# Query projections of batches 2 and 3 as three float32r products, and a newly searched issue order

## The chip, the cores and the metric

The kernel runs on one core of one Trainium2 chip. The metric is device microseconds of one execution; three executions of the kernel before took 582.05, 582.50 and 582.72 us (median 582.5).

## The reference, cut to what matters

Three layers follow one another, on 4 batches of 576 positions (2304 tokens of 512 numbers), all in float32.

1. Performer attention, 8 heads of 64, taken in 4 pairs of heads per batch. With `proj = x @ omega.T` (128 features) each of q and k becomes `exp(proj - max)`. For k the maximum is taken per position over the features and then `kv = k_p.T @ v`; for q too, and the output is `q_p @ kv` over its normalizer.
2. A dense layer: `h = x @ w_in`, `g = h * clip(h + 3, 0, 6) / 6`, `x = g @ w_out` (512 to 2048 to 512).
3. A mixture of 8 experts (512 to 1024 to 512, one expert per token, many tokens skipped): `x + gate * relu(x @ w1[e]) @ w2[e]`.

The change touches the product `proj` of q in batches 2 and 3, the second product of the expert with few rows left ("small expert"), and the order of everything.

## The kernel before, in words

The attention works on pairs (b, p): batch b, heads 2p and 2p+1. A [128 x 576] tile holds the 64 numbers of the two heads on partitions 0 to 63 and 64 to 127, so each product with `wb` (omega, scaled) uses one half of the rows of TensorE's array. For one pair: `load_k`, `load_q`, `load_v` fetch it (L417 to L430); `phi_mm` (L452) projects k; `phi_max`, `phi_exp` make its features; `k_kvs` (L489) sums them with v; `q_proj` (L511 to L531) projects q, in two calls of 288 positions, each one product per head into a PSUM bank of its own; `q_copy` (L547, ACT) moves the result to SBUF; `q_max` (L555, POOL) takes the maximum over partitions, `q_sub` (L560, DVE) and `q_exp` (L564, ACT) finish the features; `x_nums` (L574), `x_div`, `x_turn` (L596) give the attention's output, and `x_hi`, `x_lo` split it into two float32r parts `xh`, `xl`.

Tiles with tag `raw` hold k and q of a pair. There are three such buffers, and in the kernel before a pair uses two.

The dense layer runs over five chunks of tokens (512, 512, 256, 512, 512) and 16 blocks f of the hidden width. `mm1(c, f)` (L716) makes 12 float32r products (xh·wh, xl·wh, xh·wl, over four slices of 128), DVE and ACT make g and split it into `gh` and `gl`, `mm2(c, f, t)` (L747) adds three products of 512 columns to an accumulator. While chunk 0 runs, `w_in` and `w_out` are converted and split by ACT and DVE (`cv_*`, L643 to L695). Batches 0 and 1 of the attention precede and accompany chunk 0; batches 2 and 3 accompany chunks 1 and 2. The expert layer stands at the end: one expert with up to 576 rows (`ga_*`, L1038 and L1070), and up to 32 rows of another, the small expert (`s_*`): `s_up` (L1173), `s_turn_r` (L1184), `s_down` (L1191 to L1197, 8 steps of 4 products, each on 32 columns of the array).

Nothing is scheduled on the chip: the program adds some 2,090 pieces of work with an engine, dependences and tiles to a planner, and a stored list of numbers, ORDER, gives the order in which they are issued; each engine takes its own pieces in that order. The planner's costs and due times only served the search for that list, and the number of idle products that keep TensorE busy in batch 0 (`fill`, L295) comes from its gaps. The lines around the change:

```python
for r in range(2):
    T.matmul(ps[r][:, 0:n], wb[half(r), :], qr[half(r), c], start=True, stop=True)
```

TensorE works in three shapes here: the full array (the dense layer, the experts, transposes), the array cut into two halves of rows (`phi_mm`, `q_proj`), and cut into strips of columns (`k_kvs`, `x_nums`, `s_up`, `s_down`). A step from one shape to another is called a turn below. The planner gives a turn 0.2 us.

Of the kernel before, what the change touches and what calls it, by code (L numbers as in the profile page):

```python
# [9 lines left out]
F32 = mybir.dt.float32  # L10
# [37 lines left out]
QPE = ()  # L48
# [3 lines left out]
MERGE = 2  # L52
VX = 2
# [200 lines left out]
def performer_moe_kernel(  # L254
# [59 lines left out]
    ones = const.tile([128, 128], BF16, name="ones")  # L314
    V.memset(ones, 1.0)

    first = const.tile([128, 1], F32, name="first")
    G.partition_all_reduce(first, idle[:, 0:1], channels=128, reduce_op=bass_isa.ReduceOp.max)
    half_t = const.tile([128, 1], F32, name="half_t")
    V.memset(half_t, 0.5)  # L320
# [1334 lines left out]
```

## Time and profile before

| | |
|---|---|
| median of three runs | 582.5 us (582.05 to 582.72) |
| the profiled execution | 580.91 us, its span 579.1 us |
| granted TensorE clock, mean | 0.997 of 2.4 GHz |
| busy: PE, DVE, ACT, POOL | 98%, 73%, 51%, 19% of the span |

The span runs from the first to the last instruction; 1.8 us of the profiled execution lie around it. PE is TensorE's stream of products, PEld its weight loads. A float32 product is issued as two instructions, a float32r product as one. The end of a product is modelled, so durations overlap; what one costs is read from the distance of starts.

### The profile page before, as it was taken

The page shows a single profiled execution, that of the slowest core. Times are in us where ns is not written, and L with a number is a line of the kernel's source. Part 1 is how long each engine was busy: PE and PEld are TensorE (multiplying, and loading weights), DVE is VectorE, ACT ScalarE, POOL GpSimd, SP SyncE. Part 2 cuts the span into 40 slices and gives each one's busy share as a digit, 9 for nine tenths or more (in the row PEclk, how much of TensorE's full clock was granted, in tenths as well). Part 3 has the DMA queues.
Part 4 walks back from the last instruction along what each step waited for, and adds up shares of the span by engine and source line. Part 5 has one row for each costly group of instructions (what it writes and reads, how often), then busy time and mean ns, then how long its engine had stood idle before and what let it go on. Part 6 is the DMA issues. An engine that isn't in the chain of part 4 may idle for free. (4 is left out here: it accounts for less than half of the span.)

```text
span 579.1 us, 11188 instructions
## 1 busy us (share of the span) xinstructions
PE 565.2 (98%) x4115; PEld 468.8 (81%) x4115; DVE 423.5 (73%) x1116; ACT 293.6 (51%) x665; POOL 109.5 (19%) x83
## 2 busy tenths in 40 slices
PE   9899999999999999999999999999999999999993
PEld 7778788888888787878988888888888888898872
DVE  5999999988652441356678886798899974599962
ACT  6999999896573533357743431321432224553310
POOL 4543023000020202023222000020020133200363
PEclk9999999999999999999999999999999999999998
DMA  8634665656465143214544243132123435264721
GB/s 329 214 112 162 206 217 184 210 187 223 163 236 153 37 136 119 60 51 124 180 140 153 74 126 100 47 92 55 37 38 105 149 93 163 85 229 133 237 65 66
DMA packets 37256, 79.52 MB, mean 137 GB/s; under 512 B 5612, under 2 KB 6252, under 8 KB 37200
## 3 DMA queue, kind: packets, MB, share of 16 engines
q1 hardware_dynamic: 35312, 74.93, 41.1%
q0 software_dynamic: 1744, 3.56, 2.0%
q8 instruction: 33, 0.54, 0.4%
q10 hardware_dynamic: 144, 0.29, 0.2%
q14 instruction: 23, 0.19, 0.1%
HBM read 63.71 MB, written 15.18 MB: 136 GB/s over the span
## 5 line engine op out<-in xcount | busy, mean ns | idle before, releaser
L747 PE MATMUL acc<-wo,gh 128*128 128x512 f32 x576 | 180.8, 395 | 0.0
L747 PEld LDWEIGHTS acc<-wo,gh 128*128 128x128 f32 x576 | 105.5, 188 | 22.1 <-issue 1.2
L767 DVE CUSTOM_DVE_ANT_0 idle<-x,wg 128x512 uint8<-128x512 f32 x162 | 112.7, 695 | 5.3 <-ACT x L753 1.5
L747 PE MATMUL acc<-wo,gl 128*128 128x512 f32 x288 | 112.3, 390 | 0.0
L555 POOL PARTITION_ALL_REDUCE mx<-pr x26 | 52.9, 2076 | 237.1 <-ACT pr L547 237.1
L731 ACT CAST gh<-g 128x512 fp32r<-128x512 f32 (+1 forms) x80 | 46.6, 584 | 97.0 <-PE acc L747 80.7
L737 DVE TENSOR_TENSOR gl<-g,gh 128x512 fp32r<-128x512 f32 (+1 forms) x80 | 51.2, 640 | 57.1 <-ACT gh L731 21.7
L722 ACT ACTIVATE g<-mm,half_t 128x512 f32<-128x512 f32 (+1 forms) x80 | 52.0, 651 | 67.7 <-DVE gl L737 36.1
L716 PE MATMUL mm<-xh,wih 128*128 128x512 f32 (+1 forms) x320 | 80.8, 374 | 0.2 <-DVE xn L587 0.2
L716 PE MATMUL mm<-xl,wih 128*128 128x512 f32 (+1 forms) x320 | 78.9, 368 | 0.0
L727 DVE SCALAR_TENSOR_TENSOR g<-g,mm 128x512 f32<-128x512 f32 (+1 forms) x80 | 49.6, 630 | 26.1 <-ACT g L722 25.8
L716 PEld LDWEIGHTS mm<-xh,wih 128*128 128x128 f32 x320 | 56.0, 188 | 11.7 <-DVE g L727 0.6
L716 PEld LDWEIGHTS mm<-xl,wih 128*128 128x128 f32 x320 | 56.9, 188 | 10.2
L747 PEld LDWEIGHTS acc<-wo,gl 128*128 128x128 f32 x288 | 54.0, 188 | 11.7
L716 PE MATMUL mm<-xh,wil 128*128 128x512 f32 (+1 forms) x256 | 61.6, 363 | 0.0
L716 PEld LDWEIGHTS mm<-xh,wil 128*128 128x128 f32 x256 | 44.9, 189 | 7.5
L845 POOL DMA_INDIRECT tab<-rec,r_sloti x18 | 19.3, 1070 | 154.5 <-DVE rec L841 150.6
L473 ACT ACTIVATE kp<-att,kmx 128x128 f32<-128x128 f32 x130 | 38.3, 390 | 7.8 <-DVE kmx L458 6.7
L458 DVE TENSOR_REDUCE kmx<-att 128x3 f32<-128x384 f32 (+1 forms) x64 | 28.8, 483 | 12.4 <-PE att L452 12.2
L560 DVE TENSOR_TENSOR pr<-pr,mx 128x576 f32<-128x576 f32 x26 | 26.1, 1005 | 1.4 <-POOL mx L555 1.3
L672 DVE CUSTOM_DVE_ANT_0 ca<-w,ca 128x1024 uint16<-128x1024 uint16 x32 | 23.6, 741 | 3.0 <-ACT w L658 2.2
L452 PEld LDWEIGHTS att<-wb,raw 64*128 64x128 f32 x260 | 19.8, 190 | 5.6 <-ACT pr L547 1.5
(222 smaller groups left out, 773.8 us busy)
## 6 DMA issues: line engine op xcount, KB each, us to landing
wil<-wils SPq DMA_DIRECT2D x64, 256.0 KB, 2.7
w<-w_in SPq DMA_DIRECT2D x16, 512.0 KB, 3.7
w<-w_out SPq DMA_DIRECT2D x16, 512.0 KB, 3.5
out<-x SPq DMA_DIRECT2D x18, 256.0 KB, 3.3
x1d<-x SPq DMA_DIRECT2D x18, 256.0 KB, 3.9
vx<-vn SPq DMA_DIRECT2D x13, 322.5 KB, 4.0
wils<-cl SPq DMA_DIRECT2D x16, 256.0 KB, 2.9
wraw<-w SPq DMA_DIRECT2D x16, 256.0 KB
```

Source lines behind the costliest of these rows:

```text
L458: V.reduce_max(out=mx[:, 0:n], in_=st[key, b, p, g, h][:, 0:n * M].rearrange("p (g m) -> p g m", m=M), axis=AX.X, negate=True)
L473: A.activation(kp[:, i], ps[:, i * M:(i + 1) * M], AF.Exp, bias=mx[:, i:i + 1], scale=1.0)
L555: G.partition_all_reduce(mx, st["e", b, p, r], channels=128, reduce_op=bass_isa.ReduceOp.max)
L560: V.tensor_sub(pr, pr, st.pop(("qm", b, p, r)))
L672: V.tensor_tensor(c, c, lo, op=ALU.add)
L716: T.matmul(po, w[:, k, :], moving(x, k, c), start=(n == 0), stop=(n == 3 * KC - 1))
L722: A.activation(t, mmp[c, f][:, 0:CHS[c]], AF.Relu, bias=half_t, scale=2.0 ** -UP / 6.0)
L727: V.scalar_tensor_tensor(out=t, in0=t, scalar=1.0, in1=mmp.pop((c, f))[:, 0:CHS[c]], op0=ALU.min, op1=ALU.mult)
L731: A.copy(gh, gt[c, f])
L737: V.tensor_sub(gl, t, gh.bitcast(F32))
L747: T.matmul(accs[c, t], g[:, ts], w[:, r, f % 2, :], start=(f == 0 and j == 0), stop=(f == FT - 1 and j == 2))
L767: V.tensor_tensor_reduce(out=idle.bitcast(mybir.dt.uint8), in0=x1[i], in1=wg[:, e, :], scale=1.0, scalar=0.0, op0=ALU.mult, op1=ALU.add, a ...
```

## The change

It does three things.

First, in batches 2 and 3 the projection of q is made of parts. `wb_hi` and `wb_lo` split `wb` once into `wbh` and `wbl`; per pair `q_hi` (ACT) rounds q to float32r and `q_lo` (DVE) takes the rest. `q_proj` then issues three float32r products per head, wbh·qh, wbl·qh and wbh·ql, instead of one float32 product, in calls of 320 and 256 positions instead of 288 and 288. `qh` and `ql` are tiles of tag `raw`, of which there are still three. So when `q_lo` runs, q, qh and ql hold all three, and `load_k` of the next pair is put behind `q_lo` (`aft`).

Second, small tiles share memory to make room for the new ones (`r_pos` with `r_d`, the list's work tiles in the buffer of `wbh`, `ea` and `ra` in one tile, and the like).

Third, ORDER is a new list. Read against the names of the pieces, the two lists differ in these points:

| | before | after |
|---|---|---|
| pieces in all; on ACT; on DVE | 2090; 557; 651 | 2108; 566; 660 |
| turns before the first `mm1` | 14 | 19 |
| turns from there to `mm1(1, 0)` | 18 | 15 |
| turns from there to the experts | 40 | 42 |
| turns in the experts' stretch | 4 | 6 |
| PE pieces ahead of the first `mm1` | 53 | 55 |
| `s_down`, 8 steps | all in a row | 3, then `ga_down(7, 2)`, then 5 |
| `wb_hi` | - | third of all pieces |
| `wb_lo` | - | at `mm1(0, 12)` |
| `table` (DVE, two memsets) | at `mm1(0, 10)` | at `mm1(1, 13)` |

Around the pairs (3, 0) and (3, 1) the new list has, on PE: `phi_mm(3,0)` first half and second half, `mm2(1,14)`, `x_nums(2,3)`, `q_proj(3,0)` twice, `route_rank`, `x_turn(2,3)`, `k_kvs(3,0)`, `phi_mm(3,1)`; on DVE, in that stretch: `q_sub(2,3)`, two `phi_max(3,0)`, `q_lo(3,0)`; on SP `load_k(3,1)` stands right behind `x_nums(2,3)`. The core of the diff, without the list:

```diff
+    wbh = sm.tile([128, M], F32R, tag="wbh", name="wbh")
+    wbl = od.tile([128, M], F32R, tag="wbl", name="wbl")
...
+        if b >= SPLIT:
+            return (slice(0, 320), slice(320, S))[i]
...
+    def wb_hi():
+        A.copy(wbh, wb)
+    def wb_lo():
+        V.tensor_sub(wbl, wb, wbh.bitcast(F32))
+    def q_hi(b, p):
+        st["qh", b, p] = at.tile([128, S], F32R, tag="raw", bufs=RAW, name="qh")
+        A.copy(st["qh", b, p], st["qr", b, p])
+    def q_lo(b, p):
+        st["ql", b, p] = at.tile([128, S], F32R, tag="raw", bufs=RAW, name="ql")
+        V.tensor_sub(st["ql", b, p], st["qr", b, p], st["qh", b, p].bitcast(F32))
...
-        if (b, p) not in QPE:
+        if b >= SPLIT:
+            qh, ql = st["qh", b, p], st["ql", b, p]
+            for j, (w, x) in enumerate(((wbh, qh), (wbl, qh), (wbh, ql))):
+                for r in range(2):
+                    T.matmul(ps[r][:, 0:n], w[half(r), :], x[half(r), c], start=(j == 0), stop=(j == 2))
+        elif (b, p) not in QPE:
...
+            add("ACT" if b + p == 0 else "SP", SPC, -9, load_k, (), seq="sraw", w=["kr"], tl=[("raw", "k")], nbytes=S * 512,
+                aft=[("ql", (b * 4 + p - 1) // 4, (p - 1) % 4)] if b * 4 + p > 4 * SPLIT else [])
...
+            fine = b >= SPLIT
+            if fine:
+                add("ACT", act(S), u, q_hi, (), r=["qr"], w=["qh"], tl=[("raw", 0), ("raw", "h")])
+                add("DVE", dve(S), u, q_lo, (), mode="x", r=["qh", "wbl"], w=["ql"], tl=[("raw", 0), ("raw", "h"), ("raw", "l")])
...
+                add("PE", 3 * (n + 32) / 2400 + 0.03 if fine else 0.62, u + i, q_proj, (i,), mode="r", r=["wb", "ql" if fine else "qr"] + ["qm", "shapes"] * mine, w=[("qps", i)],
+    sc.add("ACT", 0.22, 90.0, lambda: wb_hi(), r=["wb"], w=["wbh"])
+    sc.add("DVE", 0.2, 90.0, lambda: wb_lo(), mode="x", r=["wbh"], w=["wbl"])
```

## Rows read from the trace of the kernel before

**Rows 1.** The page's first part: busy time, share of span, instructions.

```profile
PE 565.2 (98%) x4115; PEld 468.8 (81%) x4115; DVE 423.5 (73%) x1116; ACT 293.6 (51%) x665; POOL 109.5 (19%) x83
```

**Rows 2.** Busy time by stretch: length, PE, PEld, DVE, ACT, POOL, clock, DMA share, GB/s.

```profile
0.00:20.00 20.00, 17.75 (x166) 14.54 (x168) 13.81 (x29) 14.62 (x42) 9.57 (x10) 1.00 0.86 310
20.00:40.00 20.00, 17.61 (x350) 14.60 (x348) 19.15 (x44) 18.91 (x57) 11.00 (x6) 1.00 0.48 153
40.00:60.00 20.00, 19.98 (x231) 16.64 (x227) 19.39 (x44) 19.20 (x49) 4.44 (x2) 1.00 0.50 159
...
165.00:306.00 141.00, 141.00 (x1302) 116.95 (x1300) 70.40 (x152) 71.12 (x190) 27.67 (x14) 1.00 0.39 119
...
560.00:580.00 20.00, 10.00 (x105) 8.07 (x104) 4.92 (x9) 1.48 (x4) 6.56 (x7) 0.88 0.18 65
```

**Rows 3.** Timeline of PE, first `mm1`: start us, us, engine, line, operation, tiles, count.

```profile
47.40 1.19 PE L716 MATMUL mm<-xh,wih 128*128 128x512 f32 x4
```

**Rows 4.** Timeline of PE, batch 3.

```profile
268.28 0.39 PE L747 MATMUL acc<-wo,gl 128*128 128x512 f32 x1
268.51 0.49 PE L596 MATMUL att<-ident,xn 128*128 128x128 f32 x3
268.93 1.24 PE L519 MATMUL att<-raw,wb 64*128 64x288 f32 x8
270.01 1.53 PE L452 MATMUL att<-wb,raw 64*128 64x128 f32 x20
271.47 0.28 PE L489 MATMUL att<-vx,kp 128*64 128x65 f32 x2
```

**Rows 5.** Timeline of PE around calls that stand alone, and float32 transposes on the full array.

```profile
255.04 0.62 PE L747 MATMUL acc<-wo,gh 128*128 128x512 f32 x2
255.49 0.39 PE L747 MATMUL acc<-wo,gl 128*128 128x512 f32 x1
255.81 1.24 PE L519 MATMUL att<-raw,wb 64*128 64x288 f32 x8
...
303.00 0.76 PE L519 MATMUL att<-raw,wb 64*128 64x288 f32 x4
303.69 0.74 PE L747 MATMUL acc<-wo,gh 128*128 128x512 f32 x2
...
500.04 0.99 PE L994 MATMUL att<-ident,xga 128*128 128x128 f32 x8
500.96 0.73 PE L747 MATMUL acc<-wo,gh 128*128 128x512 f32 x2
```

**Rows 6.** Timeline of PE: float32r products of 320 and of 256 columns.

```profile
540.17 0.75 PE L1038 MATMUL mm<-xl,gw 128*128 128x320 f32 x4
540.75 0.75 PE L1038 MATMUL mm<-xh,gw 128*128 128x320 f32 x4
541.34 0.62 PE L1070 MATMUL acc<-gw,grh 128*128 128x512 f32 x2
...
546.09 0.64 PE L1038 MATMUL mm<-xl,gw 128*128 128x256 f32 x4
546.57 1.12 PE L1038 MATMUL mm<-xh,gw 128*128 128x256 f32 x8
```

**Rows 7.** Instructions of L519: count, duration ns min/median/max, first and last start.

```profile
L519 PEld LDWEIGHTS att<-raw,wb x96: 182/186/188, 30.9 to 305.4; 64*128 64x128 f32 x96
```

**Rows 8.** Groups by shape, 165 to 306 us: count, busy, mean ns, idle before.

```profile
L564 ACT ACTIVATE pr<-pr 128x576 f32<-128x576 f32 x14 | 9.6, 695 | 3.8 <-DVE pr L560 3.0 <-DVE rd L585 0.7
...
L560 DVE TENSOR_TENSOR pr<-pr,mx 128x576 f32<-128x576 f32 x14 | 14.3, 1019 | 0.8 <-POOL mx L555 0.7
L737 DVE TENSOR_TENSOR gl<-g,gh 128x512 fp32r<-128x512 f32 x15 | 10.4, 691 | 24.2 <-PE acc L747 10.0 <-PE att L596 7.1 <-ACT gh L731 6.9
```

**Rows 9.** Timeline of PE, then of PEld, around the small expert's second product.

```profile
561.94 2.48 PE L1196 MATMUL acc<-ew,rT 128*32 128x128 f32 x64
564.35 0.73 PE L1070 MATMUL acc<-gw,xh 128*128 128x512 f32 x2
...
561.94 1.45 PEld L1196 LDWEIGHTS acc<-ew,rT 128*32 128x32 f32 x52
563.76 0.39 PEld L1196 LDWEIGHTS acc<-ew,rT 128*32 128x32 f32 x12 [0.37 <-issue]
```

**Rows 10.** The loads of k: time from issue to landing, and one issue on SP.

```profile
DMA to landing us min/median/max: 2.9/4.3/6.4
...
264.68 0.33 SPq L419 DMA_DIRECT2D raw<-kt  x1
```

More of the change, by code (lines that the diff above doesn't have):

```diff
@@ L52 @@
 MERGE = 2
+SPLIT = 2
 VX = 2
@@ L315, in performer_moe_kernel @@
     V.memset(ones, 1.0)
-    first = const.tile([128, 1], F32, name="first")
-    G.partition_all_reduce(first, idle[:, 0:1], channels=128, reduce_op=bass_isa.ReduceOp.max)
+    const.tile([128, 1], F32, name="even")
+    upper = const.tile([128, 1], F32, name="upper")
+    G.partition_all_reduce(upper, idle[:, 0:1], channels=128, reduce_op=bass_isa.ReduceOp.max)
     half_t = const.tile([128, 1], F32, name="half_t")
@@ L328, in performer_moe_kernel @@
     pidx = const.tile([128, 1], F32, name="pidx")
-    upper = const.tile([128, 1], F32, name="upper")
     thr = const.tile([128, NT // 128], F32, name="thr")
@@ L361, in performer_moe_kernel @@
     od = ctx.enter_context(tc.tile_pool(name="od", bufs=1))
-    od.tile([128, 56], F32, tag="pad", name="pad")
+    wbh = sm.tile([128, M], F32R, tag="wbh", name="wbh")
+    wbl = od.tile([128, M], F32R, tag="wbl", name="wbl")
+    od.tile([128, 8], F32, tag="pad", name="pad")
     at = ctx.enter_context(tc.tile_pool(name="at", bufs=1))
@@ L815, in route_copy @@
         V.tensor_copy(tot, ps[:, 64:64 + TPC[c] * NE].rearrange("p (n e) -> p n e", e=NE))
-        pos = sm.tile([128, TPC[c], NE], F32, tag="r_pos", name="r_pos")
+        pos = sm.tile([128, TPC[c], NE], F32, tag="r_d", name="r_pos")
         V.tensor_copy(pos, ps[:, 0:TPC[c] * NE].rearrange("p (n e) -> p n e", e=NE))
@@ L822, in route_slot @@
         tot, pos, oh, act = rt["tot"], rt["pos"], rt["oh"], rt["act"]
-        sm_ = sm.tile([128, TPC[c]], F32, tag="r_sm", name="r_sm")
+        sm_ = sm.tile([128, TPC[c]], F32, tag="r_mx", name="r_sm")
         V.reduce_sum(out=sm_, in_=rt["ex"], axis=AX.X)
@@ L872, in list_in @@
         j3 = bc(jdx.unsqueeze(2), LS)
-        exc = sm.tile([128, NE], F32, tag="l_exc", name="l_exc")
+        lw = lb["w"] = sm.tile([128, M], F32, tag="wbh", name="lw")
+        exc = lw[:, 3 * NL:3 * NL + NE]
         V.tensor_sub(exc, inc, nb)
@@ L883, in list_e @@
         ge, lt = lb["ge"], lb["lt"]
-        hit = sm.tile([128, NL], F32, tag="l_hit", name="l_hit")
+        lw = lb["w"]
+        hit = lw[:, 0:NL]
         V.reduce_sum(out=hit, in_=ge, axis=AX.X)
         V.tensor_mul(lt, ge, bc(eidx.unsqueeze(1), LS))
-        ei = sm.tile([128, NL], I32, tag="lb_e", name="lb_e")
-        eb = sm.tile([128, NL], F32, tag="l_eb", name="l_eb")
+        ei = lw[:, NL:2 * NL].bitcast(I32)
+        eb = lw[:, 2 * NL:3 * NL]
         V.reduce_sum(out=eb, in_=lt, axis=AX.X)
@@ L902, in list_r @@
         V.tensor_scalar(hit, hit, -float(TABN), float(TABN), op0=ALU.mult, op1=ALU.add)
-        ri = sm.tile([128, NL], I32, tag="lb_r", name="lb_r")
+        ri = lb["w"][:, 3 * NL + NE:4 * NL + NE].bitcast(I32)
         V.tensor_add(ri, eb, hit)
@@ L1207, in performer_moe_kernel @@
     ntot = sm.tile([128, 1], I32, tag="ntot", name="ntot")
-    ea = sm.tile([128, 1], I32, tag="ea", name="ea")
-    ra = sm.tile([128, 1], I32, tag="ra", name="ra")
-    es = sm.tile([128, 1], I32, tag="es", name="es")
-    rs = sm.tile([128, 1], I32, tag="rs", name="rs")
+    ear = sm.tile([128, 2], I32, tag="ea", name="ear")
+    ea, ra = ear[:, 0:1], ear[:, 1:2]
+    esr = sm.tile([128, 2], I32, tag="es", name="esr")
+    es, rs = esr[:, 0:1], esr[:, 1:2]
     lb = {}
@@ L1257, in list_b @@
         V.tensor_sub(rest, cnt, used)
-        nb = begun(rest, "b_nb")
-        lb["nb"], lb["inc"] = nb, prefix(nb, "b_inc")
+        nb = begun(rest, "a_oh")
+        lb["nb"], lb["inc"] = nb, prefix(nb, "a_t8")
     def expert_of(t):
@@ L1305, in attention, with add @@
             t = start + p * period + AT[f"o{b}{p}"]
-            def add(eng, cost, dt, f, a, r=(), w=(), tl=(), nbytes=0, seq=None, mode="f", over=()):
+            def add(eng, cost, dt, f, a, r=(), w=(), tl=(), nbytes=0, seq=None, mode="f", over=(), aft=()):
                 last = chain.get(seq)
@@ L1312, in add @@
                     chain[seq] = (seq, b, p)
-                sc.add(eng, cost, t + dt, lambda p=p: f(b, p, *a), mode=mode, o=[last] if last else [], r=[k if k in ("wb", "shapes") else (k, b, p) if isinstance(k, str) else (*k, b, p) for k in r],
+                sc.add(eng, cost, t + dt, lambda p=p: f(b, p, *a), mode=mode, o=[*([last] if last else []), *aft], r=[k if k in ("wb", "wbl", "shapes") else (k, b, p) if isinstance(k, str) else (*k, b, p) for k in r],
                        w=[(k, b, p) if isinstance(k, str) else (*k, b, p) for k in w] + list(over),
@@ L1318, in kind @@
                 return "ps"
-            add("ACT" if b + p == 0 else "SP", SPC, -9, load_k, (), seq="sraw", w=["kr"], tl=[("raw", "k")], nbytes=S * 512)
+            add("ACT" if b + p == 0 else "SP", SPC, -9, load_k, (), seq="sraw", w=["kr"], tl=[("raw", "k")], nbytes=S * 512,
+                aft=[("ql", (b * 4 + p - 1) // 4, (p - 1) % 4)] if b * 4 + p > 4 * SPLIT else [])
             add("SP", SPC, -9, load_q, (), seq="sraw", w=["qr"], tl=[("raw", 0)], nbytes=S * 512)
@@ L1356, in attention @@
                 n = c.stop - c.start
-                add("PE", 0.62, u + i, q_proj, (i,), mode="r", r=["wb", "qr"] + ["qm", "shapes"] * mine, w=[("qps", i)],
-                    tl=[("raw", 0)] + [(kind("x"), "q", r, i) for r in range(2)] + [("pr", r) for r in range(2)] +
+                add("PE", 3 * (n + 32) / 2400 + 0.03 if fine else 0.62, u + i, q_proj, (i,), mode="r", r=["wb", "ql" if fine else "qr"] + ["qm", "shapes"] * mine, w=[("qps", i)],
+                    tl=([("raw", "h"), ("raw", "l")] if fine else [("raw", 0)]) + [(kind("x"), "q", r, i) for r in range(2)] + [("pr", r) for r in range(2)] +
                     ([("qmx", g, h) for g, h in parts] if mine else []))
```

163 rows, old and new, of the table ORDER are left out of this document.

## The prediction, made before the result was known

> **What bounds the kernel.** I read the busy shares first, then the same by stretches, then TensorE's timeline where the change touches it. PE is busy for 565.2 of 579.1 us, DVE for 73% and ACT for 51% [rows 1]. By stretches there are two regimes. In the first 40 us PE sits idle for 4.6 us and spends more on idle products, while ACT and DVE are close to full from 20 us on; from 40 us to the end of the products, at about 570 us, PE hardly rests [rows 2]. The granted clock is at the upper level, 2.4 GHz, in these stretches. So from 47.4 us on, the first `mm1` [rows 3], time is what PE's stream costs: a product removed is gained, and work added to ACT or DVE costs nothing unless PE must wait for it. In batches 2 and 3 (165 to 306 us) DVE and ACT are each busy for half of the 141 us [rows 2].
>
> **1. `q_proj` in batches 2 and 3: 8 pairs, 16 calls.** Before, the eight instructions of two calls run from 268.93 to 270.01, 1.08 us [rows 4]. About 0.1 of that is the turn into half-array shape, so a call is 0.49 us and a pair 0.98. That the two heads run side by side is seen in this: twenty float32 instructions of 128 columns on half arrays (`phi_mm`) start within 1.46 us, 0.073 each with a turn in it, where eight on the full array take 0.92 us, 0.115 each [rows 4, 5].
>
> After, a call is three products on each half. The trace has no float32r product on a half array. The nearest rows are float32r products on the full array: four of 320 columns in 0.58 us, so 0.146 each, four of 256 in 0.48 us, 0.12 each [rows 6]. If the halves run side by side as they do in float32, a pair costs 3 x 0.146 + 3 x 0.12 = 0.80 us, and the saving is 8 x (0.98 - 0.80) = 1.4 us. If they don't, a pair costs twice that, 1.60 us, and the change loses 8 x 0.62 = 5.0 us. At the other end, without the overhead that full-array products show over their columns (320 columns at 2.4 GHz are 0.133 us), it is 0.72 us a pair and a saving of 2.1. I take 1.4: the float32 half-array rows are nearest in shape, and they pair.
>
> Weights could spoil this: six loads a call instead of four, and one load lasts 0.186 us [rows 7], longer than a product's 0.12. In float32 each instruction also has its own load, and pairs of them follow one another at 0.25 us with 288 columns streamed twice (0.24), so the loads cost nothing there; in `phi_mm` two loads and two products take 0.146 us with the turn behind them, about 0.13 without [rows 4]. That is about the pace that is now wanted. The Trainium skill speaks against it: its page "TensorE: Matmul & The Clock Gate", Part 3, says a weight load overlaps a running product only where the row group differs, and here each half reloads weights for every product. By that rule the load of a half would be added to each of its products. What the rows of this kernel give for it: 3 x (0.186 + 0.146) + 3 x (0.186 + 0.12) = 1.91 us a pair, 7.5 us lost. The rows above contradict it for float32, so it gets a small chance.
>
> **2. `q_hi` and `q_lo`.** Eight casts of 576 on ACT, 0.70 us each by the nearest row (an activation of 576), 5.6 us; eight subtractions of 576 on DVE, between 0.69 x 576/512 = 0.78 and 1.02 us (the same shape, while POOL works), 6 to 8 us [rows 8]. They lie beside PE in a stretch where each engine has 70 us free [rows 2]: nothing by themselves. If that cover were gone they would cost up to 14 us, but no stretch there is near it. `wb_hi` stands at the start of ACT's queue and waits for `wb` while ACT has nothing else; `wb_lo` (about 0.25 us) and the removal of two memsets from the busy part of DVE cancel.
>
> **3. The ring of three `raw` buffers.** This is the wait that the change adds. `load_k` of the next pair can't start before `q_lo` has freed q; behind it on SP stand `load_q` and the blocks of `wil`. For most pairs the list leaves 6 us or more of PE work between `load_k` and the `phi_mm` that needs it. Between `load_k(3,1)` and `phi_mm(3,1)` there are only two `q_proj` (0.80), a `k_kvs` (about 1.3), an `x_turn` and `route_rank` (0.4) and three turns: some 2.9 us. A load of k takes 2.9 to 6.4 us to land, median 4.3 [rows 10]; before, the load issued at 264.68 was used at 270.01, 5.3 us later [rows 4, 10]. If SP issues it only where the list has it, PE waits 1.4 to 2.4 us there; if `q_lo` is early, nothing. `q_lo(3,0)` itself stands in DVE's queue behind a `q_sub` that waits for POOL, and two maxima. The other bound is below nothing only through a better list, which is in part 5. I take 0.4 us over all pairs.
>
> **4. The small expert's second product.** Its 64 products take 2.41 us, 561.94 to 564.35 [rows 9]. The first 52 weight loads follow at 0.028 us each (1.45/52); then PEld stands 0.37 us for nothing that the profile shows, and the last twelve are slower too. At the first pace 64 take 1.79, with the turn at the end 1.89; so the stall costs 0.52 us. In two runs of 24 and 40 products, with three long ones (0.68 us) between, neither reaches the place where it stalled. The split costs a turn out and a turn in, 0.24 us. Net -0.28; bounds -0.52 (turns cost nothing) and +0.24 (the stall comes anyway).
>
> **5. The rest of the list.** A turn from the full array into halves costs 0.09 us ahead (0.32 from the last product to the call at 255.81, against 0.23 to 0.25 between others) and 0.1 in the first pair; a call alone between two turns takes 0.69 [rows 5]. So a turn is about 0.1 to 0.19. From the first `mm1` to the experts the list has 57 turns instead of 58: nothing. Five more stand ahead of the first `mm1`, where PE has idle time [rows 2]. There the new list puts two more PE pieces (a `k_kv` of batch 1, 1.2 us) ahead of the first `mm1`, with their share of ACT's work: it starts later by about what was done earlier. I take nothing for the start, with 2 us to either side, since 4.6 us of idle PE and the idle products can shrink or grow there.
>
> **Sum** against the profiled execution (580.91, of which 579.1 is the span): -1.4 + 0.4 - 0.3 + 0 = -1.3 us, 579.6. That execution is 1.6 us below the median of the three runs; from the median, 582.5 - 1.3 = 581.2 us. Less than 0.2%, 1.2 us, can't be told from no change in this kernel.
>
> **Rivals.**
> - *Given back.* The saving becomes waits: PE's stream gets shorter, but one wait at `phi_mm(3,1)` of 1.4 us takes the place of the 1.4. For it: the 4.3 us landing. Against: DVE is half idle and may reach `q_lo` early. 1.4 + 0.3 against 1.4 and a few tenths of turns: 582.3.
> - *Slower by the ring.* One mechanism: `q_hi`, `q_lo`, `load_k`, `phi_mm` become a chain that PE waits on pair by pair. It takes a cast (0.7), a subtraction (1.0), an issue (0.33) and a landing (4.3), 6.3 us, and it decides where the list has less than that between `q_hi` and the next pair's `phi_mm` in real time. Were it 1.4 to 2.4 us at (3,1) and as much again at one or two neighbours, say 4 us in all, the sum is -1.7 + 4 = +2.3: 584.8. For it: batch 3 packs four pairs in 60 us. Against: before, PE was busy throughout that stretch [rows 2].
> - *The halves don't pair, or loads are not hidden*: +5.0 - 0.3 + 0.4, 587.6, or with the loads 590.
> - *A shorter start.* The new list takes 2 us of the idle time before the first `mm1`: 579.2. For it: the idle time is there; against: ACT and DVE bound it, and their work is the same.
>
> **Chances.** Forecast, 580.2 to 582.2: 0.42. Given back, 0.24. Slower by the ring, 0.16. No pairing or no hiding, 0.07 (the rule's part 0.02). Shorter start, 0.11. The range 579.0 to 584.9 leaves out the no-pairing case and the edges. Faster by over 0.2% (below 581.3): two thirds of the forecast, the shorter start and a little of the rest, 0.42. Within 0.2%: 0.35. Slower: 0.23.
>
> **What would show it.** Right: the instructions of a `q_proj` pair, twelve of them, start within 0.8 to 0.9 us; PE has no wait on a load of k; `s_down` has no gap in PEld. Wrong: twelve starts in 1.6 us or more; PE waiting at `phi_mm(3,1)` for a load or for `q_lo`; the first `mm1` more than 2 us later than 47.4 us without PE work to match it. If the time is below 579, the start or the dense stretch holds a gain that I haven't seen.

## The result, and the profile after

The changed kernel takes 585.3 us, median, against 582.05 of the kernel before: a ratio of 1.0052, 95% interval [1.0037, 1.0068]. It is slower by some 3 us, where 581.2 was forecast, and just above the range, which ended at 584.9. The profiled execution takes 583.92 us with a span of 582.1, against 580.91 and 579.1.

Busy time by stretch in the profile after, with the columns of [rows 2] (length; PE, PEld, DVE, ACT, POOL; granted clock; DMA share; GB/s):

```profile
0.00:20.00 20.00, 18.35 (x202) 14.82 (x202) 14.31 (x33) 16.20 (x47) 8.60 (x9) 1.00 0.91 348
20.00:40.00 20.00, 19.02 (x371) 15.95 (x370) 17.15 (x45) 19.17 (x62) 11.73 (x6) 1.00 0.49 147
...
165.00:306.00 141.00, 137.10 (x1236) 114.57 (x1235) 101.14 (x260) 70.24 (x183) 32.70 (x18) 1.00 0.40 124
...
560.00:580.00 20.00, 12.86 (x113) 9.49 (x111) 8.49 (x25) 0.79 (x2) 9.19 (x10) 0.96 0.22 74
```

Three things are to be seen against [rows 2]. PE is idle for 2.6 us in the first 40 us, not 4.6. From 165 to 306 us, where PE was busy all the time, it now stands for 3.9 us, although it has less work there. And in that stretch DVE does 101.1 us of work in place of 70.4: gate dots, and the routing of chunk 0, which the list of before had later, now stand in it.

The first `mm1` starts at 46.74 us, 0.66 earlier than in [rows 3]; but in a second profile of the same kernel it starts at 47.18, and in the kernels below that share its start at 46.4 to 47.6. Against one profile of before, that is no sure gain. A pair of `q_proj` calls, in the timeline of PE of the kernel after (start, busy us, engine, line, tiles, shapes, count):

```profile
163.96 0.41 PE L541 MATMUL att<-qh,wbh 64*128 64x320 f32 x2
164.21 0.30 PE L541 MATMUL att<-qh,wbl 64*128 64x320 f32 x2
164.35 0.31 PE L541 MATMUL att<-ql,wbh 64*128 64x320 f32 x2
164.50 0.28 PE L541 MATMUL att<-qh,wbh 64*128 64x256 f32 x2
164.62 0.28 PE L541 MATMUL att<-qh,wbl 64*128 64x256 f32 x2
164.73 0.28 PE L541 MATMUL att<-ql,wbh 64*128 64x256 f32 x2
164.91 1.36 PE L456 MATMUL att<-wb,raw 64*128 64x128 f32 x17
```

Two products, one on each half, take 0.14 to 0.15 us together at 320 columns and 0.11 to 0.12 at 256: the halves run side by side, and six weight loads a call don't show. Only the first two take 0.25, the turn into this shape. The pair takes 0.95 us with its turn, where [rows 4] had 1.08.

What PE waits for from 225 to 306 us, in the view of waits of the kernel after (us in total, times, longest):

```profile
PE att L456 <- DVE g L752: 1.7, 1, 1.7
PE att L599 <- ACT pr L589: 1.4, 1, 1.4
PE mm L741 <- DVE g L752: 0.8, 1, 0.8
```

That is what this stretch loses, where attention and dense layer run together: 3.9 us in three waits, none of which is a load of k or `q_lo`. Each is followed back below, in the order of time.

The third line (at 237.7 us) is an `mm1` that needs a bank of PSUM which `mm1_mul` (L752) frees. The queue of DVE ahead of that `mm1_mul`:

```profile
232.11 1.56 DVE L792 CUSTOM_DVE_ANT_0 idle<-x,wg 128x512 uint8<-128x512 f32 x1
...
236.74 1.50 DVE L792 CUSTOM_DVE_ANT_0 idle<-x,wg 128x512 uint8<-128x512 f32 x1
...
238.17 1.27 DVE L752 SCALAR_TENSOR_TENSOR g<-g,mm 128x512 f32<-128x512 f32 x2
```

They are gate dots (L792), of which two take 1.5 us instead of 0.69, beside reductions on POOL (see the last section). Between them stand the two memsets of the table, 0.27 us. The second line (at 261.9 us) is `x_nums` of pair 3 of batch 2, behind `q_exp`, `q_sub` and a `q_max` on POOL. The timeline of POOL shows what that `q_max` waited for:

```profile
231.98 1.96 POOL L580 PARTITION_ALL_REDUCE mx<-pr  x1 [33.66 <-ACT pr L572]
235.99 2.53 POOL L580 PARTITION_ALL_REDUCE mx<-pr  x1 [2.04 <-DVE pr L585]
255.92 1.97 POOL L580 PARTITION_ALL_REDUCE mx<-pr  x1 [17.40 <-ACT pr L572]
260.10 1.96 POOL L580 PARTITION_ALL_REDUCE mx<-pr  x1 [2.22 <-DMA tab<-empty]
```

The empty table is filled in a buffer of tag `mx`, of which there are two, and holds it until its store to DRAM has landed. In the list of before that happened while no `q_max` was near; in the new list it happens between two of them. The first line (at 283.8 us) is `phi_mm` of the last pair, which needs a bank freed by `mm1_mul` of chunk 2. DVE's queue ahead of it, and POOL beside it:

```profile
279.58 0.18 DVE L849 TENSOR_REDUCE r_sm<-r_ex 128x4 f32<-128x32 f32 x1
...
281.26 1.13 DVE L853 TENSOR_TENSOR r_pos<-r_pos,cnt 128x8 f32<-128x8 f32 x1
...
283.25 1.08 DVE L860 TENSOR_TENSOR r_slot<-r_slot,r_act 128x4 f32<-128x4 f32 x1
...
285.24 0.41 DVE L752 SCALAR_TENSOR_TENSOR g<-g,mm 128x256 f32<-128x256 f32 x1
```

```profile
281.23 3.91 POOL L580 PARTITION_ALL_REDUCE mx<-pr  x2 [9.71 <-DVE cnt L854]
```

`route_slot` of chunk 0 stands there as one piece of 5.7 us (279.58 to 285.24). Some of its small instructions take about 1 us instead of 0.17, beside the two reductions on POOL. The same piece of chunk 1 takes 3.5 us in e2 (below), where none runs beside it. So some 2.2 of the 5.7 us come from that meeting, more than the wait of 1.7 us.

Last, the small expert's second product, in the timeline of PEld of the kernel after; [rows 9] has it before:

```profile
562.42 1.03 PEld L1223 LDWEIGHTS acc<-ew,rT 128*32 128x32 f32 x36 [0.41 <-issue]
564.03 0.18 PEld L1223 LDWEIGHTS acc<-ew,rT 128*32 128x32 f32 x4 [0.58 <-issue]
564.99 0.30 PEld L1097 LDWEIGHTS att<-gw,xh 128*128 128x128 f32 x2 [0.78 <-issue]
```

The first run of 24 goes through (560.79 to 561.58), the second stalls after 36 of its 40, twice. The 64 products take 0.79 + 2.57 = 3.36 us in place of 2.41.

### The profile page after: what moved, and what is told of

The parts are those of the page before. It is cut to its first block, busy times and chain, and to the rows that moved or that the text cites. A ratio compares the mean times of both kernels' runs of the same rounds, so it can differ in the third digit from the quotient of the medians.

```text
span 582.1 us, 11269 instructions
## 1 busy us (share of the span) xinstructions
PE 565.5 (97%) x4143; PEld 468.5 (80%) x4143; DVE 426.3 (73%) x1125; ACT 298.8 (51%) x674; POOL 107.9 (19%) x83
## 5 line engine op out<-in xcount | busy, mean ns | idle before, releaser
L792 DVE CUSTOM_DVE_ANT_0 idle<-x,wg 128x512 uint8<-128x512 f32 x162 | 117.5, 725 | 11.6 <-DMA x<-x1d 4.5
L752 DVE SCALAR_TENSOR_TENSOR g<-g,mm 128x512 f32<-128x512 f32 (+1 forms) x80 | 49.7, 629 | 27.3 <-ACT g L747 27.1
L585 DVE TENSOR_TENSOR pr<-pr,mx 128x576 f32<-128x576 f32 x26 | 21.4, 831 | 3.5 <-POOL mx L580 3.5
L678 ACT ACTIVATE w<-w 128x512 int32<-128x512 uint32 x32 | 22.8, 722 | 1.6 <-DMA w<-w_in 1.2
```

What stands on the lines that cost most here:

```text
L678: A.activation(lo, lo.bitcast(U32), AF.Copy, scale=2.0 ** -29)
L752: V.scalar_tensor_tensor(out=t, in0=t, scalar=1.0, in1=mmp.pop((c, f))[:, 0:CHS[c]], op0=ALU.min, op1=ALU.mult)
L792: V.tensor_tensor_reduce(out=idle.bitcast(mybir.dt.uint8), in0=x1[i], in1=wg[:, e, :], scale=1.0, scalar=0.0, op0=ALU.mult, op1=ALU.add, a ...
```

## The experiments

Theory A: the float32r products gain what they should; the list loses more, because gate dots, routing and the table stand in front of work that PE waits for. Rival B: the parts `q_hi` and `q_lo` themselves make PE wait. The kernels were timed beside the kernel before in four groups, on three chips: e1 to e4; f1, s1, s4 and the changed kernel again; g1 to g3; h. Across groups the ratios are to be compared. The medians, and the ratios to the kernel before on the same chip:

| kernel | us | ratio, 95% interval |
|---|---|---|
| changed, timed again | 584.4 | 1.0053 [1.0036, 1.0070] |
| e1, table early | 583.2 | 1.0030 [1.0018, 1.0041] |
| e2, gates late | 587.7 | 1.0092 [1.0076, 1.0108] |
| e3, both | 586.1 | 1.0084 [1.0071, 1.0097] |
| e4, old projection, new list | 586.5 | 1.0079 [1.0064, 1.0095] |
| f1, DVE pieces placed | 581.4 | 1.0002 [0.9993, 1.0011] |
| g1, f1 with the old projection | 582.8 | 1.0022 [1.0012, 1.0031] |
| s1, `s_down` in one run | 586.1 | 1.0086 [1.0071, 1.0100] |
| s4, `s_down` in four runs | 584.1 | 1.0046 [1.0029, 1.0064] |
| g2, f1 with a filler ahead | 583.0 | 1.0020 [1.0010, 1.0031] |
| g3, f1, four runs, four dots moved | 583.9 | 1.0030 [1.0017, 1.0043] |
| h, f1, four runs, two dots moved | 580.5 | 0.9997 [0.9987, 1.0007] |

**e1: the table early.** The list alone is changed; pieces are named in place of their numbers.

```diff
   PE mm1(0,10)
+  DVE table
...
   PE mm2(0,8,0)
+  SP table_out
...
   DVE q_sub(2,2,1)
-  DVE table
   POOL q_max(2,2,0)
...
   DVE route_max(0)
-  SP table_out
```

> The changed kernel, with only the two pieces of the empty table (its memsets on DVE and its store on SP) moved back to where the list of before has them, behind the mm1 of chunk 0, step 10. Theory A (the table sits in one of the two mx buffers until its store has landed at about 260 us, the q_max of batch 2 pair 3 waits for that buffer, and x_nums of that pair wait behind it on TensorE): the wait of 1.4 us at 261.9 us goes, the other two large TensorE waits (0.9 us at 237.7, 1.8 us at 283.8) stay; about 1.4 us less than the changed kernel, so some 1.6 us over the kernel before. Rival B (the loss is the work that the float32r parts add: q_hi and q_lo in the chain from the load of q to its projection): no more than 0.3 us changes, and the table's wait is taken over by another at the same place.

Measured 583.2, 1.5 us over before as Theory A has it. In its view of waits, 225 to 480 us, the one on `pr` is gone, and the other two stand (the one of `mm1` is shorter by 0.3 us, about what the two memsets took ahead of it):

```profile
PE att L454 <- DVE g L750: 1.7, 1, 1.7
PE mm L739 <- DVE g L750: 0.5, 1, 0.5
```

**e2 and e3: the gates late, and both.** Gate dots, their loads and the routing go back to where the list of before has them, measured by PE's work.

```diff
   PE mm2(3,5,2)
+  DVE route_slot(0)
...
   DVE mm1_mul(3,15)
+  PE route_rank(1)
+  DVE route_copy(1)
+  DVE route_slot(1)
...
   DVE mm1_mul(4,0)
   DVE mm1_lo(3,15)
   PE mm2(3,14,0)
```

> The changed kernel, with the gate dots of chunks 0 and 1, the loads of x1 for them and the routing of chunks 0, 1 and 2 moved back to the same TensorE work as in the list of before (they had come forward by 25 to 50 us into batches 2 and 3); the two x1 copies of chunk 2 go along, to keep the buffers in order. Theory A (gate dots and the routing stand in DVE's queue ahead of mm1_mul and of the maxima): the waits of 0.9 us at 237.7 and of 1.8 us at 283.8 go, the one of 1.4 us at 261.9 stays; about 2.6 us less than the changed kernel, some 0.4 us over before. DVE's busy time from 165 to 306 us falls from 101 to some 75 us and rises by as much from 306 to 480 us, without new waits, as in the kernel before. Rival B (q_hi and q_lo): the waits stay, at most 0.5 us changes. Rival C (the later stretch gives it back): the waits go but 306 to 480 us is longer by as much.

> Both moves of the two kernels above in one. Theory A: all three waits go, some 4 us less than the changed kernel, so about 1 us under the kernel before: the 1.4 us that the projection saves, the start that is shorter by 0.7 us, less the 1.1 us that the tail lost at s_down. Rival B: within 0.8 us of the changed kernel.

The forecast failed, in the way of rival C. Up to 306 us it held: the two waits are gone (DVE is busy for 48.5 us from 225 to 306, 65.3 in the kernel after, and PE stands there for 0.2 us). The third was expected to stay in e2, and it is all but gone too, although the table is as late as in the changed kernel. The second reduction of that pair, in e2:

```profile
258.71 1.96 POOL L577 PARTITION_ALL_REDUCE mx<-pr  x1 [0.96 <-DVE pr L582]
```

The table still holds one of the two buffers, so this reduction waits for `q_sub`, 0.96 us, where in e1 the two follow each other without a pause. But the store has landed by then: it left at 255.54 us, in the changed kernel at 255.97. So the late table costs 1.4 us only where its store lands late.

Two new waits follow. The view of waits of e2, 225 to 480 us, and DVE's timeline ahead of the longer one:

```profile
PE acc L769 <- DVE gl L759: 4.0, 2, 2.5
```

```profile
421.42 0.69 DVE L759 TENSOR_TENSOR gl<-g,gh 128x512 fp32r<-128x512 f32 x1 [6.46 <-PE acc L769]
...
424.13 0.19 DVE L837 COPY r_tot<-att 128x32 f32<-128x32 f32 x1 [1.42 <-PE att L831]
...
424.34 0.18 DVE L846 TENSOR_REDUCE r_sm<-r_ex 128x4 f32<-128x32 f32 x1
...
427.82 0.68 DVE L749 SCALAR_TENSOR_TENSOR g<-g,mm 128x512 f32<-128x512 f32 x1
```

DVE had been idle for 6.46 us; then `route_copy` and `route_slot` of chunk 1, 3.7 us together (`route_slot` alone 3.5), came just ahead of an `mm1_mul` and of the `mm1_lo` that PE's next products needed. It is the wait of 283.8 us at another place: the same kind of piece in front, with DVE far from full. The second wait, from 459.1 us, is `route_slot` of chunk 2 ahead of an `mm1_lo`. e3 shows the same two waits. Behind the longer one the clock fell in both profiles, for which see below; that cost 1.7 us more.

**e4: the old projection in the new list.**

```diff
-SPLIT = 2
+SPLIT = 4
...
-        if b >= SPLIT:
+        if b >= 2:
             return (slice(0, 320), slice(320, S))[i]
```

> The changed kernel and its list, but the projections of q in batches 2 and 3 as float32 products again (one product for each half in the same blocks of 320 and 256 columns), without the q_hi and q_lo pieces. Theory A (the float32r products save 1.4 us of TensorE work and their parts are hidden): slower than the changed kernel by 1.0 to 1.4 us, some 4 us over before, with the three waits still there. Rival B (q_hi and q_lo cause the waits): the waits shrink by more than 2 us in sum, and the time is 1 us or more below the changed kernel's.

586.5, 1.2 and 2.1 us over the two medians of the changed kernel (585.3 and 584.4); by the ratios some 1.5. Rival B falls for the two waits on `g`: with no `q_hi` and no `q_lo` they stand in its view at 1.7 and 0.6 us. The third is 0.3 us instead of 1.4: as in e2, the store has landed in time, and the second reduction waits 1.01 us for `q_sub`. So e4 doesn't tell what `q_hi` and `q_lo` do to that wait; e1 takes it away with both in place.

**f1: DVE's pieces placed.** From e1, `route_slot` of chunk 0 and its stores go behind the attention of batch 3, and 22 gate dots and `route_rank` move by some places.

```diff
-  DVE route_slot(0)       (ahead of q_copy(3,1,..))
...
   DVE mm1_mul(2,15)       (behind the attention of batch 3)
+  DVE route_slot(0)
+  POOL route_put(0,3)
+  POOL route_put(0,1)
...
```

> The kernel with the table early, and 27 more pieces moved: the slot piece of chunk 0's routing and its four stores behind the attention of batch 3, behind a stretch in which TensorE doesn't wait for DVE, and 21 gate dots of chunks 0 to 2 by some places each, so that none stands ahead of an mm1_mul that TensorE waits for. Theory A (DVE's queue: gate dots ahead of mm1_mul at 238 us, 5.7 us of routing ahead of mm1_mul at 284 us; the two late waits of the kernel with the gates late came from the slot pieces standing ahead of mm1_mul there): all three large waits between 225 and 306 us go, no wait over 1 us follows up to 480 us, and the time is 3 to 4 us under the changed kernel: about 581, from 0 to 1.5 us under the kernel before. Rival B (DVE is simply full, whatever the order; a wait that goes comes back elsewhere): no better than the kernel with the table early alone, 583.2.

581.4, 2.9 us under the changed kernel timed beside it, and level with before. Its waits from 225 to 480 us, and its stretch from 165 to 306 us:

```profile
PE att L597 <- ACT pr L587: 0.4, 1, 0.4
```

```profile
165.00:306.00 141.00, 140.45 (x1312) 118.06 (x1314) 98.75 (x239) 71.80 (x186) 27.71 (x14) 1.00 0.40 126
```

DVE does 98.75 us there, nearly as much as in the kernel after, and PE stands for 0.55 us instead of 3.9. So what cost the time was not how much DVE had to do but what stood where in its queue: Theory A, for the dense stretch. One thing f1 leaves together. The new places also take `route_slot` away from the reductions on POOL that lengthened it by 2.2 us. e2 shows that an undisturbed `route_slot` makes PE wait as well; how much of the 3.9 us the place alone would cost was not tried.

**g1: f1 with the old projection**, by the edit of e4.

> The kernel with its DVE pieces placed, but the projections of q in batches 2 and 3 as float32 products again, in the same blocks of 320 and 256 columns, without q_hi and q_lo. Here no large wait hides or adds anything, so this measures the first part by itself. Theory A: 1.0 to 1.6 us slower than the kernel with its pieces placed (581.4), about 582.8. Rival B (q_hi and q_lo cost as much as the products save): within 0.4 us of it, or faster.

582.8 against f1's 581.4. The ratios to before, 1.0022 and 1.0002, put the float32r products at some 1.2 us, with 0.4 to 1.9 as an estimate from the two intervals. In g1 a pair runs from 164.93 to 166.01, 1.08 us; in f1 from 163.93 to 164.88, 0.95. That alone is 8 x 0.13 = 1.0 us; pairs whose two calls stand apart have more turns.

**The changed kernel again, and the clock.**

> The changed kernel itself once more, for its median beside these kernels on the same chip and for a second profile. Its runs fell into two groups, at 583.8 to 584.4 and at 585.3 to 586.4 us, with a mean granted clock of about 0.997 and 0.995. Theory E (after the wait of 1.8 us at 284 us the clock is sometimes granted at half for some 3 us, as the profile of the old projection in the new list shows at 286 us): if the profile is of the upper group, the granted clock is 0.50 right behind that wait, and the products from 286 us take twice as long. Rival: the granted clock is lower elsewhere or all through.

584.4. This profile has no halved clock in the middle, so it doesn't show the theory; that of s1 (below), which has the same wait, does. Its stretches behind the wait, with the columns of [rows 2]:

```profile
286.00:288.00 2.00, 1.74 (x9) 1.43 (x10) 2.00 (x6) 1.29 (x4) 1.66 (x2) 0.77 0.44 149
288.00:290.00 2.00, 2.00 (x10) 1.90 (x10) 1.85 (x5) 1.76 (x5) 1.48 (x2) 0.50 0.03 4
290.00:292.00 2.00, 2.00 (x17) 2.00 (x17) 0.99 (x4) 1.10 (x3) 0.97 (x1) 0.87 0.16 25
```

In the changed kernel 19 products lie in 288 to 290 us at a clock of 1.00; here 10, at 0.50, the lower level of 1.2 GHz. By the shares, 2 x (0.23 + 0.50 + 0.13) = 1.7 us of work is lost. The same shows in e4 behind its wait of 1.7 us (0.50 from 286 to 288), in e2 and e3 behind the ones of 2.5 us (0.67 from 428 to 432; 0.50 from 428 to 430) and in g3 behind one of 2.3 us (0.50 from 550 to 552). In these profiles, then, the clock fell behind each of the three waits of 2.3 to 2.5 us and behind two of the six of 1.7 us (in e4 and s1, not in the changed kernel, the same again, e1 and s4). So a wait of this length costs itself, and in some profiles 1.7 us more.

**s1 and s4: the small expert's second product in one run and in four.**

```diff
 s1                          s4
-  s_down 0, 1, 2               s_down 0, 1
   ga_down(7,2)               + ga_down(6,1)
+  s_down 0, 1, 2               s_down 2, 3
   s_down 3 to 7                ga_down(7,2)
                                s_down 4, 5
                              + ga_down(7,1)
                                s_down 6, 7
```

> The changed kernel, with s_down in one run of 64 products again (its first three pieces moved back behind ga_down 7,2). Theory A (two runs cost two more turns and the second run stalls more than the one run did): TensorE's losses from 560 us on fall from 2.0 to about 0.9 us, the time by about 1.1 us, to some 584.2. Rival D (the stall falls at a moment, at about 563.4 us in both kernels, and not after so many products): it stands at the same moment and costs as much, the time falls by 0.3 us at most, the price of the turns.

> The changed kernel, with s_down in four runs of 16 products, with three long ga_down products (0.68 us) between each two. Theory A (the stall comes after some 35 to 50 short products in a row, that is, when TensorE has used up the instructions that lie ready, and long products let them come up again): no stall within any run, the losses from 560 us on are those of the turns alone, some 1.2 us (two more turns than the changed kernel, without its 1.2 us of stalls); the time is 0.6 to 0.9 us under the changed kernel. Rival D (a moment, not a count): one of the later runs stalls by 0.5 us or more, and the time is up to 0.6 us over the changed kernel.

s1 was not faster: 586.1, where 584.2 was expected; in its profile the halved clock explains about 1.7 us of that. Its run stalls twice, after 55 and after 59 products, by 0.6 us each. PEld at the run's first and at the next load behind it:

```profile
563.46 1.45 PEld L1221 LDWEIGHTS acc<-ew,rT 128*32 128x32 f32 x51 [0.41 <-issue]
...
567.01 0.30 PEld L1095 LDWEIGHTS att<-gw,xh 128*128 128x128 f32 x2 [0.20 <-issue]
```

The 64 products in one run take 3.55 us here, where one run took 2.41 in the kernel before. So in the new list they are slower with the split and without it. In s4 no run stalls; its PEld timeline, the first and the third of four equal runs:

```profile
560.49 0.38 PEld L1221 LDWEIGHTS acc<-ew,rT 128*32 128x32 f32 x16 [0.42 <-issue]
...
563.36 0.38 PEld L1221 LDWEIGHTS acc<-ew,rT 128*32 128x32 f32 x16 [0.41 <-issue]
```

What stands ahead of each run is the turn. The time, 584.1, can't be told from the changed kernel's 584.4, where 0.6 to 0.9 us less was expected. A run that begins at 563.36 us goes through here, and s1's stalls are at 565.3 and 566.1, so it isn't a moment (rival D).

**g2: 64 more products ahead of everything.**

```diff
-            for _ in range(... if spare[1] else OPEN):
+            for _ in range(... if spare[1] else 0):
                 T.matmul(ps[:, 0:128], idle, idle, start=True, stop=True)
+            for _ in range(0 if spare[1] else OPEN + 64):
+                T.matmul(ps[0:8, 0:8], ones[:, 0:8], ones[:, 0:8], start=True, stop=True)
```

> The kernel with its DVE pieces placed, and at the start, while TensorE waits for its first load, 71 idle products of 8 rows and 8 columns (bf16) in place of the first 7 idle float32 products: 64 products more ahead of everything. Theory F (TensorE's instructions come in blocks: 33 packets and 0.54 MB on the instruction queue for 8,286 of TensorE's products and weight loads, so one packet for some 128 products; the stall falls where the last packet begins, near product 4,090, which lies in s_down): s_down is now products 4,098 to 4,164, the block's edge lies ahead of it among long products, and the stalls of 0.55 and 0.61 us in s_down go; the losses from 560 us on fall by about 1 us, the time to about 580.5. Rival A (a count of short products in a row): the stalls stay in s_down, after as many of its products. Rival D (a moment): likewise. If the idle products delay the first real one, the start is longer by that, to be seen ahead of 20 us.

Theory F falls. The stalls stand where f1 has them, after 24 + 27 and 24 + 31 products of `s_down`, while by the records 57 more products stand ahead. PEld in f1, then in g2:

```profile
559.41 0.59 PEld L1221 LDWEIGHTS acc<-ew,rT 128*32 128x32 f32 x24 [0.41 <-issue]
560.15 0.17 PEld L1221 LDWEIGHTS acc<-ew,rT 128*32 128x32 f32 x4
560.88 0.14 PEld L1221 LDWEIGHTS acc<-ew,rT 128*32 128x32 f32 x3 [0.56 <-issue]
561.62 0.25 PEld L1221 LDWEIGHTS acc<-ew,rT 128*32 128x32 f32 x9 [0.60 <-issue]
```

```profile
562.00 0.59 PEld L1223 LDWEIGHTS acc<-ew,rT 128*32 128x32 f32 x24 [0.41 <-issue]
562.76 0.16 PEld L1223 LDWEIGHTS acc<-ew,rT 128*32 128x32 f32 x4 [0.17 <-issue]
563.49 0.17 PEld L1223 LDWEIGHTS acc<-ew,rT 128*32 128x32 f32 x4 [0.57 <-issue]
564.24 0.20 PEld L1223 LDWEIGHTS acc<-ew,rT 128*32 128x32 f32 x8 [0.58 <-issue]
```

Over all profiles the stalls come after some 51 to 63 short products, and three long ones between don't start that count anew, while long ones behind every 16 prevent them. What runs out there was not settled. The filler delayed the start, so g2's time says nothing on the stall.

**g3 and h: the tail.** In f1 a `ga_down` waits 0.6 us at 540 us for `ga_rl`, which stands behind gate dots.

```diff
   DVE gate_dot(15,1)
-  DVE gate_dot(15,4)           (g3)
-  DVE gate_dot(16,4)           (g3, h)
-  DVE gate_dot(17,1)           (g3, h)
   DVE ga_rl(4,0)
+  DVE gate_dot(16,4), (17,1)   (h)
-  DVE gate_dot(15,8)           (g3)
   DVE ga_rl(5,0)
+  DVE gate_dot(15,4), (16,4), (17,1), (15,8)   (g3)
```

> The kernel with its DVE pieces placed, s_down in four runs of 16 products, and four gate dots of the last chunk moved behind ga_rl 5,0, which ga_down 4,1 waits for (0.6 us at 540 us); the rank product of chunk 0's routing a few places earlier. Expected: no stall in s_down (0.3 to 0.6 us less from 560 us on), the wait at 540 us gone (0.5 us): about 580.4, 0.9 us under the kernel before. If the four runs' turns cost what the stalls did, 580.9.

> The kernel with its DVE pieces placed, s_down in four runs of 16 products, and only two gate dots of the last chunk (16,4 and 17,1) moved from ahead of ga_rl 4,0 to behind it, where they stay ahead of ga_rl 5,0, so that DVE doesn't stand idle there and ga_wl (1,6) comes no later than with its pieces placed. Theory A (order on DVE's queue, and the count of short products): the wait of 0.6 us at 540 us goes without the one of 2.3 us at 546 us that the move of four dots brought, no stall stands in s_down; 581.4 less 0.3 to 0.9 us, so about 580.8, 0.5 us under the kernel before. Rival B: another wait of the same size follows in the tail, 581.4 or more.

g3 failed, with 583.9 where 580.4 was expected: that wait went, and another came. Its one wait from 500 us on:

```profile
PE acc L1095 <- DVE gw L1055: 2.3, 1, 2.3
```

DVE stood idle for 1.34 us ahead of `ga_rl(5,0)`, and the weights' low parts (L1055) came later by that and by the dots behind it. The lowered clock behind this wait is told above. In h the wait at 540 us is gone and one of 0.6 us on the same weights remains. h takes 580.5 against 580.9 of before on the same chip (580.8 was expected): the fastest version here, and not to be told from the kernel before.

## Why the prediction was wrong

**Part 1 (1.4 us saved): right.** The halves pair and the loads are hidden; g1 against f1 gives some 1.2 us, and the pairs alone 1.0. The term of the turn was small by some 0.05 us a pair: 0.95 us with it, where 0.80 and 0.1 were reckoned. The rule of the Trainium skill ("TensorE: Matmul & The Clock Gate", Part 3) that was weighed there would have 0.18 us for each load added to each product; two products with their two loads in 0.12 to 0.15 us contradict it.

**Part 2 (`q_hi`, `q_lo` cost nothing): right.** 0.67 us a cast and 0.75 a subtraction; e4 has the same waits on `g` without them, and f1 has them without a wait of more than 0.4 us.

**Part 3 (0.4 us for the ring): no such wait.** Neither the forecast's wait nor the rival's chain on `load_k` shows in any profile here.

**Part 4 (-0.28 us): wrong, and outside its bounds.** The 64 products took 0.95 us more than before, and with the turns it is 1.1 us, where -0.28 was forecast. Two steps failed. "Neither reaches the place where it stalled" took the stall to belong to a run, but three products between don't end it. And the 2.41 us of the kernel before was taken for the price of one run in the new list too, where s1 has 3.55. Why the same run stalls longer there was not found.

**Part 5 (the rest of the list: nothing): this step failed.** I counted the turns of PE and the pieces ahead of the first `mm1`, and for DVE I read a share: busy for half of 141 us, so room for anything. A share says nothing of the place. The list put 30.7 us of DVE work into that stretch, at two places ahead of an `mm1_mul` whose bank PE needed, and the table's buffer between two `q_max`. That is 3.9 us of waits, where the whole gain was 1.4; f1, with nearly the same work on DVE in another order, has 0.4. The meeting with POOL was in sight too: `q_sub` stands in [rows 8] with 1.02 us, and part 2 priced it as that for `q_lo`, but I didn't ask what it does to a piece ahead of an `mm1_mul`. The tail got a wait of 0.6 us for `ga_rl` that before hasn't. The start was 0.66 us shorter in the first profile and 0.2 in the second, within the bounds given and within what profiles of the same start differ by.

**The rivals.** "Slower by the ring" had the side and nearly the size, with another mechanism: that its 584.8 lies near the measured 585.3 is luck. The prediction held against it that PE was busy throughout that stretch before, and this is what the new list undid.

**What stays open.** f1 is only level with before, although it has the gain of the products. An estimate, from PE's start-to-start times less the mean pace of products of the same shape in a row: f1's profile gains about 1.4 us on the products, about 1 ahead of 47 us and about 1 from there to 225 us; it loses about 2.5 us from 225 to 306 us and 2.0 from 500 on. The tail's loss is in the waits and stalls shown. Of the 2.5 us a wait is 0.4; there are 27 turns where before has 22, which at 0.1 to 0.19 us a turn would be 0.5 to 1.0; the rest is open. Which of the timed runs of the changed kernel had the halved clock can't be read from their mean clocks either: the profile timed again has a mean of 0.994 and no halved stretch in the middle.

## What to carry to other kernels

When a list is searched anew, compare engine by engine which pieces moved across which, before reading any share: a piece of several us on an in-order queue costs whatever waits behind it, even on an engine that is half idle. Look also at what another engine does beside a moved piece: the same piece took 3.5 us alone and 5.7 beside reductions on POOL. Look for each buffer that a moved piece holds until a DMA has landed, and who takes the next one of its tag. A run of short products stalled here after some fifty of them; long products behind every 16 removed the stall, behind the first 24 alone they did not.

## What the runs showed of the hardware

A DVE instruction that reads two tensors from SBUF and starts just after a PARTITION_ALL_REDUCE begins on POOL ends about 0.9 us later than it would: a gate dot takes 1.56 against 0.69 (at 232.11 us, POOL from 231.98), an instruction on eight elements 1.13 against 0.17 (at 281.26, POOL from 281.23). Then DVE goes on within the reduction, which takes 1.96 us. In the profile of before the same falls on `q_sub` (mean 1.02 us, [rows 8], 0.75 undisturbed). A `phi_max`, which reads one tensor, from PSUM, isn't lengthened: 0.55 us at 269.73, POOL from 269.48. And it goes both ways: a gate dot that began 0.08 us into the reduction of 235.99 took its usual time, 0.63, and the reduction took 2.53 us. The Trainium skill ("SBUF — State Buffer", "SBUF: two separate sides") has the pair of ports that the two share as a lock: a DVE instruction with two SBUF inputs and a GpSimd operation that reads SBUF exclude each other, and whichever starts first holds it for the whole instruction. The trace agrees on which instructions are held up, and that either may be; but DVE's two-input instructions go on after some 1.1 us of the 1.96, not at the end.

In g2 the first twenty real products took 2.50 us in place of f1's 1.78 and the next eight 2.29 in place of 1.24, behind 71 idle products of eight columns and an idle PE of 1.23 us, in place of seven products of 128 that end as the real ones begin; the granted clock reads 1.00 in both. Why was not tried.
